# A's halves into the rows of G by transfers inside SBUF, and POOL's list in another order

## The chip, the cores and the metric

One core of a Trainium2 chip runs the kernel. The number compared is device time in microseconds of one execution on that core. The engines are PE (matrix products), DVE (vector), ACT (scalar), POOL (GpSimd) and SP, which here only issues DMA. Each has its own list of instructions in a fixed order, and they meet at semaphores.

## The reference

Two parts follow each other: a linear recurrence over 768 steps for 32 (batch, head) pairs with a 40 by 40 state, and a mixture of four causal attention experts on its output.

```python
for t in range(S):                       # S = 768, state is (B, H, 40, 40)
    y[:, :, t] = einsum('bhd,bhde->bhe', rt, state)
    Sa = einsum('bhde,bhe->bhd', state, at)
    state = state * wt[:, :, None, :] - einsum('bhd,bhe->bhde', Sa, bt)
    state = state + einsum('bhd,bhe->bhde', vt, kt)
...
logits = x @ w_gate                      # x is y, heads side by side; the two best of 4 experts per row
scores = (q @ k.T) / 8, causal           # per expert, then softmax, @ v, @ wo[e], weighted and summed
```

## The kernel before, in words

**The recurrence** takes 24 chunks of 32 steps. In a chunk the dependence between the steps is a triangular system per head: products of A (the input a times running decays) with KB (k and b over running decays) give a matrix G, and the part of G that couples the steps is inverted. Four chunks together are a wave, W = 0 to 5. A chunk's 32 heads are two units of sixteen heads, so a wave has 8 units and the recurrence 48. One turn n of the main loop (line 519) issues the stages g, k, f, p, u, y, v, t, d of units n, n-1 and n-2, in nine slots 0 to 8 (`MAIN`). After each slot come the extra jobs that the tables name for this turn and slot.

**Preparing a wave** (`prep`, table `SIDE`): a wave has 4 pieces, i = 4W + 0 to 3. In the table `2b` means step b of piece 2, a key is the turn relative to n0 = 8(W-1), and a slash goes to the next slot. The steps are a (scan of the decays into SUF, DVE), c and s (reciprocal and second scan into SC, DVE), x (A into AB, DVE), k or p (KB, on DVE or on POOL), m and n (G's products on PE and their masking by DVE into rows 0 to 63 of the tile GL), o (DMA of part of G to the scratch `Ld` in DRAM), d and q (the two halves of A into rows 64 to 103 of GL), and w, v, e (loads). Only piece 3 has its KB on POOL.

**Inverting a wave** (`invert`, table `INV`): L loads `Ld` back into MT in another layout, C writes a diagonal, T8 means eight operations of the elimination. Its 60 operations (30 products into TP, 30 sums into MT, L311) run on POOL alone for W = 1 to 5. A, D and E are DVE transposes of MT into TT (columns 0 to 15, 16 to 23 and 24 to 31). L stands in turn 8(W-1), E in turn 8W, and stage u of unit 8W is the first that reads wave W's TT.

**The order around the change.** L of wave W+1 stands on SP behind the o steps of turn 8W-1, two loads and four stores xT of the stage d of unit 8W-2. SP issues in order and keeps eight semaphores in turn for its transfers, so the ninth waits for the first to land. GL, MT and TT have two buffers each, AB four. The masking of step n, D, stage d and E stand on DVE in that order.

**After unit 47** the experts' part (`moe`, from about 375 us on) runs; the change touches nothing in it.

Of the kernel before, what the change touches and what calls it, by code (L numbers as in the profile page):

```python
# [8 lines left out]
AF = mybir.ActivationFunctionType  # L9
# [7 lines left out]
NW, NG, C = 6, 4, 32  # L17
# [16 lines left out]
    -6: "1b///0x//1k 0v 2ac//1we",  # L34
    -5: "///0m/1x 2s//1v",
    -4: "2b///1m/2k/2x/2we",
    -3: "///2m/3ac/3s 2v/3w",
    -2: "3b///0no 1no/3p/3x 3ve",
    -1: "///3m 2no 3no/0d///0q",
    0: "////1d////1q",  # L40
    2: "////2d",
    3: "////2q",
    4: "////3d",
    5: "////3q",
}

INV = {0: "L///////C", 1: "T8", 2: "T8", 3: "T8", 4: "T8", 5: "T8", 6: "T4/////A", 7: "T16/////D", 8: "E"}
INV1 = {0: "L C T10", 1: "T10", 2: "T10", 3: "T10", 4: "T10", 5: "T10", 6: "A", 7: "/////D", 8: "E"}


# [45 lines left out]
def recurrence(tc, ctx, I, xT, CM, early, tail=None):  # L96
    nc = tc.nc
# [4 lines left out]
    V, A, T, PL = nc.vector, nc.scalar, nc.tensor, nc.gpsimd  # L102
# [16 lines left out]
    def ring(name, shape, n):  # L119
        return [sp.tile(shape, F32, name=f"{name}{i}") for i in range(n)]  # L120

    A.dma_start(CM, I["CM"])
    def product():
        return ps([128, 4, 2, 32])
# [13 lines left out]
    GF = [ep.tile([128, 4098], F32, name="GLe")] + ring("GL", [128, 4098], 1)  # L138
    GL = [t[:, 0:4096].rearrange("p (g n s t) -> p g n s t", g=4, n=16, s=2) for t in GF]
# [29 lines left out]
    def load_e(i, k):  # L169
        if i < 24:  # L170
            t = (E8[i] if i < 8 else own[i % 2])[k]
            src, c0 = (("EA", 0), ("EA", 528), ("EK", 0))[k]
            nc.sync.dma_start(t[0:104], I[src][i, :, c0:c0 + t.shape[1]])

    def zero(t):
        p = t.start_partition()
        z = CM[p:p + t.shape[0], 194:195]
        for _ in t.shape[2:]:
            z = z.unsqueeze(1)
        A.activation(t, z.to_broadcast(t.shape), AF.Copy)  # L180
# [21 lines left out]
        PL.memset(t[:, 1024:1026], 0.0)  # L202

    def zgl(i):
        zero(GL[i][96:128].rearrange("p g n s t -> p (g n s t)"))

    def rest(x):
        if x < 2:
# [21 lines left out]
    def prep(i):  # L230

        w, g = divmod(i, NG)
        ab, sc, kb, pc = ABr[i % 4], SC[i % 12], KB[i % NKB], PC[i % 12]
        gl = GL[w % 2]
        SUF = SUFs[1 if i in (1, 3, 5, 7) else 0]
        sv = SUF[:, 1:529].rearrange("p (n c) -> p n c", c=33)
        EW, EA, EK = (x[0:104] for x in (E8[i] if i < 8 else own[i % 2]))
        ea = EA.rearrange("p (n c) -> p n c", c=32)
        def f0a():
            V.tensor_tensor_scan(SUF[:, 0:528][:, ::-1], EW[:, ::-1], d1[:, ::-1], 1.0, op0=OP.mult, op1=OP.add)  # L240
        def f0b():
            A.activation(pc, sv[:, ::4, 0], AF.Copy)
        def f0c():
            V.reciprocal(D1P[:, 0:528:132], sv[:, ::4, 0])
        def f1():
            V.tensor_tensor_scan(sc.rearrange("p n c -> p (n c)"), EW, D1P, 0.0, op0=OP.mult, op1=OP.add)  # L246
        aa = ab[0:104, 0:512].rearrange("p (n c) -> p n c", c=32)
        bd = ab[0:104].rearrange("p (s n c) -> p s n c", s=2, c=32)
        def f2():
            if i < 8:  # L250
                V.tensor_tensor(aa, ea, sc[:, :, 0:32], op=OP.mult)
                return
            for s in range(2):
                q = slice(64 * s, 64 * s + 40)
                V.tensor_tensor(bd[q, s], ea[q], sc[q, :, 0:32], op=OP.mult)
        def fk(e):
            e.tensor_tensor(kb[0:104].rearrange("p n (k c) -> p n k c", k=2), EK.rearrange("p (n k c) -> p n k c", n=16, k=2),  # L257
                             sv[:, :, None, 1:33].to_broadcast([104, 16, 2, 32]), op=OP.mult)
        def f5(s):
            o, q = gl[64:104, g, :, s, :], slice(64 * s, 64 * s + 40)  # L260
            a = aa[q] if i < 8 else bd[q, s]
            if True:
                A.activation(o, a, AF.Copy)
            else:
                PL.tensor_copy(o, a)
        def mm(c):
            p_a = product()
            o = gl[0:64, g].rearrange("q (p c) s t -> q p c s t", p=4)
            for p in range(4):
                for x in range(2):  # L270
                    n = p * 4 + c + x
                    if i < 8:
                        for s in range(2):
                            q = slice(64 * s, 64 * s + 40)
                            T.matmul(p_a[64 * s:64 * s + 64, p, x], kb[q, n, :], aa[q, n, :], start=True, stop=True, tile_position=(64 * s, 64 * s))  # L275
                    else:
                        T.matmul(p_a[64 * x:64 * x + 64, p], kb[0:104, n, :], bd[:, :, n], start=True, stop=True, tile_position=(0, 64 * x))  # L277
            for x in range(2):
                V.tensor_tensor(o[:, :, c:c + 2, x] if i < 8 else o[:, :, c + x], p_a[64 * x:64 * x + 64],
                                maskn[x][:, None, None, :].to_broadcast([64, 4, 2, 32]), op=OP.mult)  # L280
        def f6():
            for s in range(2):
                b = 64 * (g % 2) + 32 * s + 16 * (g // 2)
                nc.sync.dma_start(Ld[w % 2][b:b + 16].rearrange("n j t -> j n t"), gl[32:64, g, :, s])
        def load(k):
            load_e(i + (1 if k == 1 else 2), k)
        return dict(a=f0a, b=f0b, c=f0c, s=f1, x=f2, p=lambda: fk(PL), k=lambda: fk(V), d=lambda: f5(0), q=lambda: f5(1),
                    m=lambda: mm(0), n=lambda: mm(2), o=f6, w=lambda: load(0), v=lambda: load(1), e=lambda: load(2))

# [171 lines left out]
    for W in range(1, NW):  # L461
        n0 = 8 * (W - 1)
        inv = invert(W)
        for r, line in SIDE.items():
            if W == 1:
                break
            for k, part in enumerate(line.split("/")):
                for z in part.split():
                    at(n0 + r, 0 if n0 + r < 0 else k, *[P[4 * W + int(z[0])][x] for x in z[1:]])
                    if z[1] in "mn":  # L470
                        full.add(n0 + r)
        for r, line in (INV if W > 1 else INV1).items():
            for k, part in enumerate(line.split("/")):
# [5 lines left out]
    def seq(line):  # L479
        for z in line.split():  # L480
            if z[0] == "E":
                for k in (0, 2, 1)[:2 if z == "E9" else 3]:
                    load_e(int(z[1:]), k)
            elif z[0] == "Y":
                zero(ABr[int(z[1])][:, 0:512])
            elif z[0] == "W":
                rest(int(z[1]))
            elif z[0] == "Z":
                zgl(int(z[1]))
            elif z[0] == "V":  # L490
                for k in (0,) if z[2] == "0" else (2, 1):
                    load_c(int(z[1]), k)
            elif z[0] == "k":
                turned(0, int(z[1]))()
            elif z[0] == "g":
                units[int(z[1])]["g"]()
            elif z[0] in inv:
                inv[z[0]](*[int(x) for x in [z[1:]] if x])
            else:
                run(int(z[0]), z[1:])  # L500
# [18 lines left out]
    for n in range(NU + 2):  # L519
# [10 lines left out]
        for s, (x, d) in order:  # L530
            if x == "k":
                q, g = divmod(n + 2, 4)
# [466 lines left out]
```

## Time and profile before

| | |
|---|---|
| median of 3 runs | 611.88 us (607.84 to 613.04) |
| the profiled execution | 610.82 us, span 609.2 us |
| busy: PE / DVE / ACT / POOL | 515.2 / 430.9 / 426.9 / 370.5 us |
| main loop's turns 8 to 39 | about 129 to 335 us |
| DMA packets | 65230, of them 30440 under 512 B |

Times in a profile are microseconds from the start of the span. Below, list W is wave W's elimination on POOL, and E(W) the DVE transpose that closes it. In turn 8W-1 step m of piece 3 of wave W+1 is written 3m. The page's bytes per packet do not tell which transfers have short rows: here they are the o steps, whose rows are 128 bytes.

### The profile page before, as it was taken

The numbers are of one execution on the slowest core, as the hardware profiler recorded it, in microseconds if no ns is written. First come the engines' busy times: TensorE is split into PE (matmuls) and PEld (weight loads), VectorE is DVE, ScalarE is ACT, GpSimd is POOL, SyncE is SP. The second block draws the span as 40 slices with busy tenths as digits, with TensorE's granted clock in tenths as the row PEclk, the third lists the DMA queues.
The fourth block names the chain that finished last, engine by engine and source line by source line (L and its number), as shares of the span: only waits on it lengthen the run. The fifth ranks groups of instructions, "written<-read, shape, count | busy, mean of one in ns | idle before, by whom it ended". The sixth has DMA issues, their size and how long they took to land.

```text
span 609.2 us, 20123 instructions
## 1 busy us (share of the span) xinstructions
PE 515.2 (85%) x7985; PEld 441.8 (73%) x7985; DVE 430.9 (71%) x925; ACT 426.9 (70%) x1008; POOL 370.5 (61%) x597
## 2 busy tenths in 40 slices
PE   4656489988868868886998988799999999999996
PEld 4645377777757757675777777789887878897884
DVE  8666858889948966895665464787785677567752
ACT  6973167779839965893887774587776577677773
POOL 3412189818985994898488461486964566373841
PEclk9555578999969996997999999999999999999999
DMA  7864324577546646643632863442131132202101
GB/s 205 215 161 126 89 63 123 150 193 185 133 105 177 167 103 161 182 114 84 198 94 80 230 178 92 131 116 64 51 114 38 52 90 60 59 2 64 45 33 49
DMA packets 65230, 69.68 MB, mean 114 GB/s; under 512 B 30440, under 2 KB 51176, under 8 KB 65128
## 3 DMA queue, kind: packets, MB, share of 16 engines
q1 hardware_dynamic: 64984, 68.22, 41.9%
q8 instruction: 65, 1.06, 0.8%
q14 instruction: 37, 0.30, 0.2%
q10 hardware_dynamic: 144, 0.10, 0.1%
HBM read 50.99 MB, written 11.01 MB: 102 GB/s over the span
## 4 chain that ended last, share of the span: by engine, by line
PE 42%; POOL 26%; DVE 14%; issue 6%; ACT 5%; DMA 5%; SPq 1%; DVEq 0%; POOLq 0%; ACTq 0%
POOL MT L311 12%; POOL TP L311 11%; PE ot L875 6%; PE sc L829 5%; PE py L414 4%; PE pt L753 4%; PE pt L857 4%; DMA MT<-Ld 4%; PE pt L886 4%; PE pt L772 3%; PE pu L275 2%; PE pb L277 2%; PE pb L275 2%; PE pb L380 2%; DVE SC L246 1%
## 5 line engine op out<-in xcount | busy, mean ns | idle before, releaser
L311 POOL TENSOR_TENSOR MT<-MT,TP 128x30 f32<-128x30 f32 (+9 forms) x150 | 99.8, 665 | 11.8
L311 POOL TENSOR_TENSOR TP<-MT 128x30 f32<-128x30 f32 (+9 forms) x150 | 94.6, 631 | 11.1
L849 POOL TENSOR_TENSOR P<-P,m 128x128 f32<-128x128 f32 (+2 forms) x96 | 88.1, 939 | 3.4
L414 PE MATMUL py<-R,LS 128*40 128x80 f32 x1536 | 76.5, 242 | 4.6 <-DVE R L407 1.4
L838 ACT ACTIVATE P<-P,m 128x128 f32<-128x128 f32 (+2 forms) x96 | 63.8, 665 | 18.6 <-DVE m L836 14.0
L836 DVE CUSTOM_DVE_ANT_0 P<-sc,MK 128x128 f32<-128x128 f32 (+2 forms) x96 | 59.3, 623 | 23.1 <-PE sc L829 11.6
L414 PEld LDWEIGHTS py<-R,LS 128*40 128x40 f32 x1536 | 62.2, 121 | 16.5 <-ACT LS L443 9.2
L393 ACT ACTIVATE R<-pu 32x320 f32<-32x320 f32 x96 | 41.1, 428 | 42.7 <-PE pu L390 41.0
L829 PE MATMUL sc<-ks,qs 128*128 128x384 f32 (+4 forms) x256 | 61.0, 343 | 1.7 <-DVE m L836 1.6
L407 DVE TENSOR_TENSOR R<-pb,CM 64x256 f32<-64x256 f32 x96 | 40.3, 420 | 26.3 <-PE pb L404 20.4
L857 PE MATMUL pt<-CM,P 128*128 128x128 f32 x336 | 52.0, 275 | 0.9 <-ACT pt L863 0.4
L845 POOL TENSOR_TENSOR m<-m,gg 128x2 f32<-128x2 f32 x48 | 10.3, 215 | 69.5 <-DVE m L844 57.9
L363 ACT ACTIVATE LS<-pk 64x320 f32<-64x320 f32 x96 | 41.5, 432 | 8.9 <-PE pk L358 7.3
L857 PEld LDWEIGHTS pt<-CM,P 128*128 128x128 f32 x336 | 39.8, 140 | 6.0 <-ACT pt L863 1.5
L829 PEld LDWEIGHTS sc<-ks,qs 128*128 128x128 f32 x256 | 40.3, 189 | 4.4 <-DVE m L836 3.4
L753 PE MATMUL pt<-xh,wq 128*128 128x384 f32 x192 | 40.5, 344 | 2.6 <-DVE pt L861 1.2
L875 PE MATMUL ot<-pt,vv 128*64 128x256 f32 (+1 forms) x384 | 41.6, 359 | 0.1
L443 ACT ACTIVATE LS<-pt 40x320 f32<-40x320 f32 x92 | 39.6, 430 | 2.2
L863 ACT ACTIVATE pt<-pt 128x512 f32<-128x512 f32 (+1 forms) x64 | 34.3, 539 | 8.8 <-PE pt L857 7.8
L382 ACT ACTIVATE GT<-pb,OWN 128x160 f32<-128x160 f32 x96 | 32.4, 389 | 11.5 <-PE pb L380 10.9
L277 PE MATMUL pb<-AB,KB 104*64 104x64 f32 x512 | 25.4, 256 | 17.0 <-POOL KB L257 14.2
L404 PE MATMUL pb<-RB,VU 128*64 128x64 f32 x768 | 33.2, 230 | 4.2 <-ACT VU L399 3.2
(165 smaller groups left out, 1227.0 us busy)
## 6 DMA issues: line engine op xcount, KB each, us to landing
EK<-in_EK SPq DMA_DIRECT2D x20, 416.0 KB
ks<-ks SPq DMA_DIRECT2D x32, 192.0 KB
R<-in_VG SPq DMA_DIRECT2D x24, 208.0 KB
EW<-in_EA SPq DMA_DIRECT2D x20, 214.5 KB
R<-in_VT SPq DMA_DIRECT2D x48, 80.0 KB
R<-in_RT SPq DMA_DIRECT2D x24, 160.0 KB
RB<-in_RB SPq DMA_DIRECT2D x48, 80.0 KB
xT<-XT SPq DMA_DIRECT2D x48, 80.0 KB
```

The source lines that it names most:

```text
L311: return [lambda: e.tensor_tensor(tmp, row, col, op=OP.mult), lambda: e.tensor_tensor(o, o, tmp, op=OP.add)]
L363: A.activation(LS[(c + k) % 3][0:64, 8 * g:8 * g + 8], p_k[64 * k:64 * k + 64], AF.Copy)
L393: A.activation(r2[32:64, 40 * h0:40 * h0 + 640].rearrange("q (z p e) -> q z p e", z=2, p=2)[:, :, x], PU[64 * x:64 * x + 32, :, 0:160], AF ...
L407: V.tensor_tensor(o[:, :, x], p_f[64 * x:64 * x + 64], mask[x][:, None, None, :].to_broadcast([64, 4, 2, 32]), op=OP.mult)
L414: T.matmul(py[64 * s:64 * s + 40, p // 4, p % 4], ls[:, h, :], m, start=True, stop=True, tile_position=(0, 64 * s))
L753: T.matmul(p, w, x, start=(j == 0), stop=(j == len(prs) - 1))
L829: T.matmul(ps[:, c, 0:cw], QS[b][:, e, o], KS[b][:, e, z, k], start=(z == 0), stop=(z == 1))
L836: V.tensor_tensor_reduce(pv, ps[:, 0:ch, 0:cw], MK[:, 768 - n:768].rearrange("p (c k) -> p c k", c=ch), 1.0, 3e38, OP.add, OP.min, m[:, 0, ...
L838: later(DE, lambda: A.activation(P[:, 0:n], P[:, 0:n], AF.Exp, bias=m[:, 0, t:t + 1], scale=-1.0, accum_out=m[:, 1, t:t + 1]))
L849: PL.tensor_tensor(P[:, 0:n], P[:, 0:n], m[:, 3, t:t + 1].to_broadcast([128, n]), op=OP.mult)
L857: T.transpose(p[:, 128 * y:128 * y + 128], st["P"][t][:, 128 * c:128 * c + 128], ident)
L875: T.matmul(po[h, 128:256] if one else po[h], VV[b][:, k, 2 * ep + s], P[:, 256 * k:256 * k + (128 if one else 256)], start=(k == 0), stop= ...
```

## The change: what it does

Step d and step q of every piece from 8 on (two for each of 16 pieces, 32 in all) become one DMA each, from AB into rows 64 to 103 of GL, on SP, where ACT copied. Each moves 40 partitions of 16 rows of 32 floats, so 640 rows of 128 bytes. The two halves of a piece are issued together, in turns n0-1 to n0+2 instead of n0-1 to n0+5. KB of piece 3 moves from turn n0-2 to n0-3, and the elimination is dealt out in sevens and a nine. `zgl` writes the same region under another name for it.

```diff
@@ SIDE
-    -3: "///2m/3ac/3s 2v/3w",
-    -2: "3b///0no 1no/3p/3x 3ve",
-    -1: "///3m 2no 3no/0d///0q",
-    0: "////1d////1q",
-    2: "////2d",
-    3: "////2q",
-    4: "////3d",
-    5: "////3q",
+    -3: "///2m/3ac/3s 2v/3w/3p",
+    -2: "3b///0no 1no//3x 3ve",
+    -1: "///3m 2no 3no//0d 0q",
+    0: "/////1d 1q",
+    1: "/////2d 2q",
+    2: "/////3d 3q",
 }
-INV = {0: "L///////C", 1: "T8", 2: "T8", 3: "T8", 4: "T8", 5: "T8", 6: "T4/////A", 7: "T16/////D", 8: "E"}
+INV = {0: "L///////C", 1: "T7", 2: "T7", 3: "T7", 4: "T7", 5: "T7", 6: "T9/////A", 7: "T16/////D", 8: "E"}
@@ def zgl(i):
-        zero(GL[i][96:128].rearrange("p g n s t -> p (g n s t)"))
+        zero(GF[i][96:128, 0:4096])
@@ def f5(s):
             o, q = gl[64:104, g, :, s, :], slice(64 * s, 64 * s + 40)
-            a = aa[q] if i < 8 else bd[q, s]
-            if True:
-                A.activation(o, a, AF.Copy)
+            if i < 8:
+                A.activation(o, aa[q], AF.Copy)
             else:
-                PL.tensor_copy(o, a)
+                nc.sync.dma_start(o, bd[q, s])
```

On POOL, in the middle of list 2 (KB is the one product of EK and SUF; the last number of a row is its shape). Before:

```order
L311 TENSOR_TENSOR TP<-MT_121 128x234
L311 TENSOR_TENSOR MT_121<-MT_121,TP 128x18x13
...
L311 TENSOR_TENSOR MT_121<-MT_121,TP 128x22x9
L257 TENSOR_TENSOR KB_113<-EK_89,SUF_91 104x1024
L311 TENSOR_TENSOR TP<-MT_121 128x184
```

And now:

```order
L308 TENSOR_TENSOR TP<-MT_121 128x234
L255 TENSOR_TENSOR KB_113<-EK_89,SUF_91 104x1024
L308 TENSOR_TENSOR MT_121<-MT_121,TP 128x18x13
L308 TENSOR_TENSOR TP<-MT_121 128x228
...
L308 TENSOR_TENSOR MT_121<-MT_121,TP 128x22x9
L308 TENSOR_TENSOR TP<-MT_121 128x184
```

KB stood behind 44 of the 60 operations and stands behind 35. The same holds in lists 3 and 4. In list 1 all 60 stand ahead of KB in both kernels, and list 5 has no KB.

On SP, around the load of MT for wave 4 (Ld is step o, R and RB are inputs of the units, EW and EK of the next wave's pieces). Before:

```order
L284 DMA Ld_139<-GLe 32x16x32 x4
L345 DMA R_131<-in_VT 32x640
L343 DMA R_129<-in_VG 32x1664
L433 DMA xT<-XT_135 40x4x128 x4
L295 DMA MT_120<-Ld_139 128x1024
L347 DMA R_131<-in_VT 32x640
```

And now:

```order
L281 DMA Ld_139<-GLe 32x16x32 x4
L262 DMA GLe<-AB_114 40x16x32 x2
L342 DMA R_131<-in_VT 32x640
L340 DMA R_129<-in_VG 32x1664
L430 DMA xT<-XT_135 40x4x128 x4
L292 DMA MT_120<-Ld_139 128x1024
L262 DMA GLe<-AB_115 40x16x32 x2
L344 DMA R_131<-in_VT 32x640
```

The first pair of a wave stands between step o and the load of MT, the second right behind that load; the other two follow in the next two turns. PE's and DVE's orders stay as they were, and ACT's loses the 32 copies.

## Rows read from the trace of the kernel before

**Rows 1.** The page, section 4: the chain that ended last, by line.

```profile
POOL MT L311 12%; POOL TP L311 11%; PE ot L875 6%; PE sc L829 5%; PE py L414 4%; PE pt L753 4%; PE pt L857 4%; DMA MT<-Ld 4%; PE pt L886 4%; PE pt L772 3%; PE pu L275 2%; PE pb L277 2%; PE pb L275 2%; PE pb L380 2%; DVE SC L246 1%
```

**Rows 2.** Stretches: busy us of each engine, granted clock, DMA share, GB/s; units 16 to 23.

```profile
183.00:238.00 55.00, 45.52 (x942) 38.01 (x939) 43.09 (x72) 41.08 (x97) 43.11 (x62) 0.91 0.58 146
```

**Rows 3.** Waits: engine, line waited for, us in total, times, longest.

```profile
PE pb L277 <- POOL KB L257: 14.2, 3, 5.0
```

**Rows 4.** The chain of waits, 218 to 246 us: start, us, what.

```profile
227.30 2.13 POOL KB L257
...
233.46 2.31 PE py L414 x32
...
239.61 4.63 DMA MT<-Ld
...
244.28 0.16 POOL MT L297
```

**Rows 5.** The chain of waits, 121 to 136 us, one wave earlier.

```profile
121.60 0.69 PE pb L277 x16
...
124.63 1.26 PE py L414 x32
...
130.71 4.59 DMA MT<-Ld
```

**Rows 6.** Timeline of PE: start, us, instruction, [idle before <-releaser]; two starts of 3m.

```profile
174.64 1.98 PE L277 MATMUL pb<-AB,KB 104*64 104x64 f32 x32 [4.96 <-POOL KB L257]
...
229.48 1.98 PE L277 MATMUL pb<-AB,KB 104*64 104x64 f32 x32 [4.95 <-POOL KB L257]
```

**Rows 7.** Timeline of POOL: ends of lists and starts of lists.

```profile
135.34 0.15 POOL L297 MEMSET MT<- 128x32 f32 x1 [13.81 <-DMA MT<-Ld]
...
164.86 0.61 POOL L311 TENSOR_TENSOR TP<-MT 128x234 f32<-128x234 f32 x1
...
181.99 0.26 POOL L311 TENSOR_TENSOR MT<-MT,TP 128x30 f32<-128x30 f32 x1
...
189.82 1.32 POOL L311 TENSOR_TENSOR MT<-MT,TP 128x30 f32<-128x30 f32 x1
...
291.28 0.26 POOL L311 TENSOR_TENSOR MT<-MT,TP 128x30 f32<-128x30 f32 x1
299.03 0.16 POOL L297 MEMSET MT<- 128x32 f32 x1 [7.49 <-DMA MT<-Ld]
...
334.22 0.27 POOL L311 TENSOR_TENSOR MT<-MT,TP 128x30 f32<-128x30 f32 x1
```

**Rows 8.** Timeline of DVE: E(2), SUF of piece 3, two maskings, E(4), E(5).

```profile
182.99 0.65 DVE L313 STREAM_TRANSPOSE TT<-MT 128x256 f32<-128x256 f32 x1
...
214.22 1.26 DVE L240 TENSOR_TENSOR_SCAN SUF<-EW,D 104x528 f32<-104x528 f32 x1
...
218.11 0.86 DVE L407 TENSOR_TENSOR R<-pb,CM 64x256 f32<-64x256 f32 x2 [0.58 <-PE pb L404]
...
224.65 0.42 DVE L407 TENSOR_TENSOR R<-pb,CM 64x256 f32<-64x256 f32 x1 [0.64 <-PE pb L404]
...
292.28 0.65 DVE L313 STREAM_TRANSPOSE TT<-MT 128x256 f32<-128x256 f32 x1
...
334.52 0.63 DVE L313 STREAM_TRANSPOSE TT<-MT 128x256 f32<-128x256 f32 x1 [1.29 <-POOL MT L311]
```

**Rows 9.** Timeline of SP: the step o ahead of the load of MT for wave 2.

```profile
124.42 2.04 SPq L284 DMA_DIRECT2D Ld<-GLe  x4
```

**Rows 10.** L263, the copies: engine, count, ns min/median/max, first and last start.

```profile
L263 ACT ACTIVATE GLe<-AB x24: 626/627/631, 10.1 to 269.3; 40x512 f32<-40x512 f32 x24
```

**Rows 11.** Stretches: with four transfers of step o alone, and after a stall of PE.

```profile
165.00:169.00 4.00, 3.66 (x85) 2.96 (x75) 3.86 (x7) 3.23 (x8) 3.69 (x5) 1.00 0.44 77
229.00:236.00 7.00, 6.33 (x99) 5.59 (x100) 2.73 (x7) 2.35 (x5) 6.06 (x14) 0.50 0.65 147
```

**Rows 12.** The chain of waits, 60 to 75 us: landing of step o.

```profile
65.87 1.87 DMA Ld<-GL
```

## The prediction

> **What bounds the kernel now.** I read the chain of waits first. Its two longest lines are the elimination on POOL [rows 1], so in the recurrence it is the lists that must be followed, not the busiest engine: in units 16 to 23 no engine is busy for more than 46 of 55 us [rows 2]. The chain between 218 and 246 us shows why a wave takes about 55 us. POOL reaches KB at 227.30, behind 44 operations; PE's 3m starts when KB is done; the load of MT is issued at 239.61, and the next list starts at 244.28 [rows 4]. The table of waits says what the units lose there: PE waits for this KB three times, 14.2 us in all [rows 3], in lists 2, 3 and 4. PE's timeline dates it: 3m was ready at 174.64 - 4.96 = 169.68 and at 229.48 - 4.95 = 224.53 [rows 6]. The last views are POOL's and DVE's timelines, for a second bound behind the first. List 2 runs from 135.34 to 182.25, and E(2) starts at 182.99, only 0.74 us later; list 4 ends at 291.54 and E(4) starts at 292.28 [rows 7, 8]. E needs the last operation of its list, and unit 8W's stage u needs E. So the units arrive when POOL has just finished. Once E did wait: E(5), 1.29 us for POOL [rows 8].
>
> **The change, part by part.**
>
> *KB earlier.* Nothing is saved on POOL; KB and its 60 operations remain, in another order. After the memset of list 2 the 35th operation ended at 165.47, that is 30.1 us later [rows 7]; KB takes 2.13 [rows 4], so it would be done 32.3 us after a list starts, in list 2 at about 167.6, ahead of the 169.68 at which 3m wants it. PE's wait goes, in all three lists. What is late next is E: units that come 5 us earlier meet a list that ends no earlier.
>
> *The path after it.* It goes through every second wave: list 2, E(2), units 16 to 23, load, list 4, E(4), units 32 to 39, E(5). Its terms, all from rows:
> - List 2 starts at 135.34 and lasts 46.91, KB included, wherever in it KB stands [rows 7].
> - The wait for its semaphore and E itself, 0.05 + 0.65 = 0.70 [rows 8].
> - From the end of E(2), 183.64, to 3m ready, 224.53: 40.9 [rows 6, 8].
> - From 3m to the load of MT: 9.11, from 121.60 to 130.71, where PE had not been stalled [rows 5]. Behind the stall it is 10.13 today [rows 4, 6].
> - From the load's issue to the memset of list 4: 4.65 [rows 4, 5].
> - List 4 lasts 291.54 - 244.28 = 47.26 [rows 4, 7]; then 0.70 again.
> - From the end of E(4), 292.93, to where E(5) wants to run, 334.52 - 1.29 = 333.23: 40.3 [rows 8].
>
> These add up to 325.87 for the start of E(5), against 334.52: **8.65 us earlier, before costs**. Lists 3 and 5 are beside this path: list 5 starts at least when list 4 ends, where today POOL idles 7.49 us for the load [rows 7], so its end moves further forward than the units do and E(5) no longer waits.
>
> *PE's clock.* With E late, PE idles before stage u of units 16 and 32 instead of before 3m. After today's stall of 4.95 us the granted clock is 0.50 from 229 to 236 us [rows 11], its lower level, 1.2 GHz, and stage y takes 2.31 us there against 1.26 at full clock [rows 4, 5]. It could cost nothing if the waits come out shorter, or about 2 us if a second stage y falls into it. I take 1.05 for each of the two waits: **2.1**.
>
> *The 32 transfers.* A piece's pair has 2 x 640 = 1280 rows of 128 bytes. Step o moves such rows: four transfers, 2048 rows, filled 0.44 of 4 us of the 16 DMA engines, 1.76 us [rows 11]. The pair at that rate is 1.1 us of all engines. On SP it adds two issues of 2.04 / 4 = 0.51 us [rows 9]. The first pair of a wave stands between step o and the load of MT. It could delay that load by nothing, where SP waits for the XT of stage d anyway, or by two issues and two whole landings of 1.87 us [rows 12], 4.8 us. I take 1.1, since the nearest row is that of step o. The path holds two such loads, of waves 2 and 4: **2.2**. The second pair is issued behind the load and should not slow it; the other pairs have two turns or more before AB is written again.
>
> By the Trainium skill's "DMA: Bandwidth & Descriptors", section "Specifications", rows under 512 bytes fall to read-modify-write and lose the line rate. The 128-byte rows of step o agree in so far as they go at 256 KB in 1.76 us, 149 GB/s. If a write into SBUF paid twice what step o pays, the pair would be 2.2 us and the sum 2.2 us worse; no row here shows such a write.
>
> *KB beside DVE's scans.* In list 3 KB would be reached at about 184.5 + 30.1 = 214.6 (3m at 169.68, then 9.11, 1.1 and 4.65), but SUF of piece 3 ends 31.84 us after E(2) [rows 8], at 184.05 + 31.84 + 1.05 = 216.9. So POOL waits some 2 us, harmless beside 7 us of slack, and KB then starts just ahead of DVE's second scan of that piece. A POOL operation that takes 0.27 us alone took 1.32 beside a two-input operation of DVE [rows 7]: the two engines hold each other up. The scan may lose nothing, or nearly all of KB's 2.13. DVE waits 0.58 and 0.64 for PE later in the same stretch [rows 8] and wins these back, so I take 2.13 - 0.2 (its head start) - 1.2: **0.7**.
>
> The Trainium skill's "SBUF — State Buffer", section "Who interferes with whom", has it harder: VectorE with two SBUF inputs and GpSimd take a shared port in turn, and whoever starts first keeps it for its whole instruction. The 1.32 agrees. By that alone, with nothing won back, the sum would be 1.2 us worse.
>
> *ScalarE's copies.* 32 copies of 627 ns [rows 10] go, 20.1 us of ACT. ACT is busy 41 of 55 us [rows 2] and the path above runs through POOL, DVE and PE; I count **nothing**. The units' dependence hides it; if ACT alone were the path, it would be worth up to 20 us.
>
> **Sum:** 8.65 - 2.1 - 2.2 - 0.7 = 3.65 us. The profiled execution took 610.82 (span 609.2, 1.6 around it) and would take 607.2; it lies 1.06 under the median of the runs, 611.88, so I forecast **608.2**.
>
> **Rivals.**
> - *The costs don't arise.* The pairs drain while SP waits for XT, PE's clock holds, DVE loses nothing: 611.88 - 8.65 = 603.2, with a little left 604. For it: each of the three bounds above reaches down to nothing. Against it: PE idled about as long today and its clock did fall. 22%.
> - *The list is no bound, and all three waits are won:* 611.88 - 14.2 = 597.7; also if ACT's 20 us lie on the path. Against it: E(5) waited for POOL, and E(2) and E(4) start 0.74 us after their lists. 5%.
> - *The wait only changes its name.* E takes the whole of it and the clock the rest: 611.9. 10%.
> - *Slower: the first pair in front of the load of MT.* The place is SP between step o and that load, the price 4.8 us or more instead of 1.1, paid in waves 2 and 4. 8.65 - 2.1 - 0.7 - 9.5 = -3.7: 615.5. It decides from 2.9 us per load; over 1% needs 6. For it: DMA is busy for 0.65 of the stretch in which the load is issued [rows 11], and the pair's rows are short. Against it: step o's own rows. 13%.
>
> By the Trainium skill's rule on short rows alone ("DMA: Bandwidth & Descriptors", section "Specifications") this last case is half way reached, 2.2 of 4.8 us; the rows of step o, which are as short, keep it at 13%.
>
> The forecast itself, 606 to 611, has 50%.
>
> **The numbers.** About 1%, 6.1 us, is what a measurement of this kernel can tell from no change. Faster by more: the first two rivals and the forecast's edge, 0.30. Slower by more: the worse part of the last, 0.08. The rest, 0.62. The range, 602 to 613.5, takes in the whole gain at its low end and a delay of 3.5 us per load at its high end.
>
> **What would show it.** In the profile after: PE's wait for KB gone; instead DVE's L313 waits for POOL 4 to 7 us ahead of E(2) and E(4) and 1 to 3 ahead of E(3); list 4 starting 2 to 4 us earlier than 244.28; ACT down by 20 us; a slow-clock stretch of PE behind E(2). I am wrong if E never waits, if the load of MT is issued later than 9 to 11 us after 3m, or if a load's landing grows well beyond 4.6 us.

## The result: no gain, half a per cent slower

The changed kernel takes 614.73 us (median of 14 runs, 611.41 to 619.81), the kernel before 611.89 in the same comparison: ratio 1.0052, interval 1.0026 to 1.0077. The forecast was 608.2, with a range up to 613.5. Medians are of all runs, ratios and intervals of the fast runs alone, so a ratio need not be the quotient of two medians. The profiled execution after took 612.1 us, its span 610.3; it lies 2.6 under the median. Lines of the changed kernel are numbered two or three lower: L308 is the elimination on POOL, L310 the transposes D and E, L255 KB, L238 SUF, L253 AB, L262 the transfers, L292 the load of MT.

The page after, its busy times (share of the span, instructions), and the first entries of the chain that ended last by line:

```profile
PE 514.9 (84%) x7985; PEld 442.9 (73%) x7985; DVE 432.3 (71%) x925; ACT 406.6 (67%) x976; POOL 365.1 (60%) x597
...
PE ot L872 6%; PE sc L826 5%; PE pt L750 4%; PE pt L854 4%; PE py L411 4%; PE pt L883 4%; POOL MT L308 4%; POOL TP L308 3%; PE pt L769 3%; PE pb L377 2%; DVE R L423 2%; ACT LS L440 1%; DVE P L833 1%; ACT GT L379 1%; DMA MT<-Ld 1%
```

ACT fell by 20.3 us, the 32 copies. The two elimination lines held 23% of the chain before [rows 1] and hold 7% now: for most of the recurrence the list has stopped being what is waited for. The table of waits after (engine, line waited for, us, times, longest) says what took its place. PE's wait for KB [rows 3] is not in it. E's wait for its list has grown from 1.3 us, and the waits for two loads are new (before, 0.4 and 0.8 us):

```profile
DVE TT L310 <- POOL MT L308: 7.9, 2, 5.1
DVE AB L253 <- DMA EA<-in_EA: 7.7, 6, 3.1
DVE SUF L238 <- DMA EW<-in_EA: 4.5, 3, 2.3
```

DVE now waits for the loads of the pieces' inputs, EW and EA. Its timeline shows the two largest of list 3:

```profile
200.45 1.29 DVE L238 TENSOR_TENSOR_SCAN SUF<-EW,D 104x528 f32<-104x528 f32 x1 [2.25 <-DMA EW<-in_EA]
...
206.84 1.90 DVE L253 TENSOR_TENSOR AB<-EA,SC 40x512 f32<-40x512 f32 x2 [2.69 <-DMA EA<-in_EA]
```

Why the loads are late stands in SP's timeline (start, us, line, transfer). First the kernel before, in the turn behind E(2), then the changed kernel in the same turn:

```profile
187.97 1.72 SPq L433 DMA_DIRECT2D xT<-XT  x4
190.33 0.33 SPq L173 DMA_DIRECT2D EW<-in_EA  x1
...
197.53 0.31 SPq L173 DMA_DIRECT2D EA<-in_EA  x1
```

```profile
187.54 0.35 SPq L292 DMA_DIRECT2D MT<-Ld  x1
187.94 1.66 SPq L262 DMA_DIRECT2D GL<-AB  x2
189.70 2.63 SPq L344 DMA_DIRECT2D R<-in_VT  x1
192.38 0.34 SPq L345 DMA_DIRECT2D R<-in_RT  x1
192.77 0.70 SPq L349 DMA_DIRECT2D RB<-in_RB  x2
193.57 1.70 SPq L430 DMA_DIRECT2D xT<-XT  x4
195.32 1.63 SPq L262 DMA_DIRECT2D GL<-AB  x2
197.05 0.64 SPq L171 DMA_DIRECT2D EW<-in_EA  x1
...
199.08 1.63 SPq L262 DMA_DIRECT2D GL<-AB  x2
200.81 3.19 SPq L171 DMA_DIRECT2D EA<-in_EA  x1
```

From 187.54 to 197.05 SP does nothing but issue, without a gap longer than 0.1 us. A transfer takes 0.8 us of SP, a pair 1.63 to 1.66 here. The issue behind two of the pairs then does not return: the load of VT takes 2.63 us and that of EA 3.19, where such issues mostly take 0.31 to 0.34. These are the second pair, right behind the load of MT, and the fourth, behind EW and EK. In waves 2 to 4 the issues behind these two took 2.0 to 3.2 us, those behind the first and third pair 0.50 to 0.72. SP did not wait for one of its eight semaphores: from 120 to 340 us, landings held it for 0.5 us in all. EW is issued 6.7 us later than before and EA 3.3 us; 2.8 us of the 6.7 are there already at the load of MT (184.78 before). In the chain of waits after (start, us, what), EW's landing is a link. So are, further on, the issues of the first pair of wave 4 and the load of MT for list 4, which lands later than the 4.63 of [rows 4]:

```profile
197.05 3.27 DMA EW<-in_EA
...
235.06 1.12 SPq L262
236.23 0.78 SPq L262
...
239.96 6.07 DMA MT<-Ld
```

### The profile page after: what moved, and what is told of

Same layout as the page of the kernel before. It is cut to its first block, busy times and chain, and to the rows that moved or that the text cites. A ratio compares the mean times of both kernels' runs of the same rounds, so it can differ in the third digit from the quotient of the medians.

```text
span 610.3 us, 20129 instructions
## 1 busy us (share of the span) xinstructions
PE 514.9 (84%) x7985; PEld 442.9 (73%) x7985; DVE 432.3 (71%) x925; ACT 406.6 (67%) x976; POOL 365.1 (60%) x597
## 4 chain that ended last, share of the span: by engine, by line
PE 36%; DVE 9%; POOL 8%; ACT 5%; issue 4%; DMA 3%; SPq 3%; DVEq 0%; ACTq 0%; POOLq 0%
PE ot L872 6%; PE sc L826 5%; PE pt L750 4%; PE pt L854 4%; PE py L411 4%; PE pt L883 4%; POOL MT L308 4%; POOL TP L308 3%; PE pt L769 3%; PE pb L377 2%; DVE R L423 2%; ACT LS L440 1%; DVE P L833 1%; ACT GT L379 1%; DMA MT<-Ld 1%
## 5 line engine op out<-in xcount | busy, mean ns | idle before, releaser
L308 POOL TENSOR_TENSOR MT<-MT,TP 128x30 f32<-128x30 f32 (+9 forms) x150 | 93.6, 624 | 11.5
L308 POOL TENSOR_TENSOR TP<-MT 128x30 f32<-128x30 f32 (+9 forms) x150 | 93.5, 623 | 11.4
L411 PE MATMUL py<-R,LS 128*40 128x80 f32 x1536 | 78.9, 246 | 11.3 <-ACT R L390 3.7
L411 PEld LDWEIGHTS py<-R,LS 128*40 128x40 f32 x1536 | 64.5, 124 | 23.5 <-ACT LS L440 7.5
L421 ACT ACTIVATE R<-py 40x320 f32<-40x320 f32 x48 | 20.7, 431 | 24.4 <-PE py L411 24.2
```

The source lines that it names most:

```text
L308: return [lambda: e.tensor_tensor(tmp, row, col, op=OP.mult), lambda: e.tensor_tensor(o, o, tmp, op=OP.add)]
L411: T.matmul(py[64 * s:64 * s + 40, p // 4, p % 4], ls[:, h, :], m, start=True, stop=True, tile_position=(0, 64 * s))
```

## The experiments

Each ratio is against the kernel before, run beside it; times from different comparisons are set against each other by ratio, where 0.001 is 0.61 us.

**The list's order alone.** The new places of KB and of the elimination's operations, with the copies on ACT in their old turns.

```diff
-    -3: "...3w",        -2: "3b///0no 1no/3p/3x 3ve",    T8 ... T4
+    -3: "...3w/3p",     -2: "3b///0no 1no//3x 3ve",      T7 ... T9
```

> Before, with KB of piece 3 one turn earlier and the elimination dealt in sevens and a nine; the 32 copies stay on ScalarE in their old turns. Theory T (the transfers hold SP: each pair's issue takes 1.6 us and the next issue up to 3.2 us, so the loads EW and EA of the next pieces land late and DVE waits 11.4 us for them in lists 2 to 4): without transfers the list's earlier KB is worth what the prediction's sum gives without its transfer term, 8.65 - 2.1 - 0.7 = 5.9 us, so about 606 us, ratio 0.990; no wait of DVE for EW or EA beyond before's. Rival L (POOL's list takes the whole gain, the transfers cost nothing): within 1 us of before, ratio 1.000, with DVE waiting at E for all that was won.

606.6 us, 0.9911 (0.9875 to 0.9946): 5.4 us faster, as expected. Its timeline of DVE, E(2), E(4) and E(5), answering to [rows 8]:

```profile
182.80 0.63 DVE L313 STREAM_TRANSPOSE TT<-MT 128x256 f32<-128x256 f32 x1 [6.31 <-POOL MT L311]
...
287.48 0.63 DVE L313 STREAM_TRANSPOSE TT<-MT 128x256 f32<-128x256 f32 x1 [5.23 <-POOL MT L311]
...
328.86 0.65 DVE L313 STREAM_TRANSPOSE TT<-MT 128x256 f32<-128x256 f32 x1
```

E waits for POOL as the forecast had it (4 to 7 us; E(3) 2.50), and E(5) starts 5.7 us earlier than before.

**The transfers alone**, in the copies' old turns, with the list as before.

```diff
-    A.activation(o, a, AF.Copy)
+    nc.sync.dma_start(o, bd[q, s])        # pieces from 8 on
```

> Before, with the 32 transfers in place of the copies in the copies' old turns, one or two a turn over seven turns; KB and the elimination as before. Theory T: single transfers hold SP half as long at a time, but the load waits appear and the wait for KB stays, part of them in parallel with it: 2 to 6 us slower, ratio 1.003 to 1.010. Rival L: as before or up to 1 us faster, ratio 0.998 to 1.000.

614.55 us, 1.0032 (1.0008 to 1.0056): slower, as expected. So the two halves of the change have opposite signs.

**The transfers on ACT's queue**, all else as changed (`A.dma_start` for `nc.sync.dma_start`).

> The changed kernel, with the 32 transfers issued by ScalarE's queue instead of SP. Theory T, if it is SP's issue time that delays the loads: SP is as free as before, so DVE's waits for EW and EA go (under 3 us of the 11.4 are left) and the time is near e_list, about 607 us, ratio 0.992; ScalarE is held 0.8 us per transfer, about what the copy took. Rival Q (it is the traffic of 20480 short rows on the DMA engines, whoever issues it): the waits stay within 2 us of the 11.4 and the time is near the changed kernel, ratio 1.003 to 1.006.

634.1 us, 1.0371 (1.0329 to 1.0412): missed. SP's issue of VT behind the load of MT was back at 0.34 to 0.46, but POOL waited 82.7 us for the loads of MT (55.5 in the changed kernel) and DVE 19.7 us for EW. The transfers of both queues take the same eight semaphores in turn, so SP now waits for what ACT issues late (it waited 10.7 us for one such transfer ahead of a load of MT). That run says nothing on the price of the transfers.

**The third and fourth pair later** in their turns, behind the issues of EW and EK (slot 8 for slot 5).

> The changed kernel, with the third and fourth pair of a wave moved to the end of their turn, so that on SP they stand behind EW and EK of that turn instead of ahead of them. Theory T: EW lands about 2 us earlier (its wait, 1.4 and 2.3 us in lists 2 and 3, goes); EA of piece 1 is still behind a pair, so 2 to 4 us better than the changed kernel, ratio to before 0.999 to 1.003. Rival Q: no change from the changed kernel, ratio 1.005.

612.85 us, 1.0000 (0.9968 to 1.0033), as expected: 3.2 us of the loss come back from the place in SP's order alone, though the interval just touches the changed kernel's.

**Copies in the transfers' turns.** The changed kernel with ACT's copies for the transfers; and two halves of it: only the first pair of a wave as transfers, only the other three.

```diff
-    nc.sync.dma_start(o, bd[q, s])
+    A.activation(o, bd[q, s], AF.Copy)    # all / g > 0 / g == 0
```

> The changed kernel with ScalarE's copies in place of the 32 transfers, in the changed kernel's turns: the two differ in the transfers alone. Theory (the transfers cost the 8 us, the new order of the list gains 5): 606 to 608, ratio 0.990 to 0.994, no wait of DVE for EW and less than 2 us of waits for EA, E waits some 14 us. Rival (the copies' new turns beside the new list cost it, not the transfers): 612 to 615, ratio above 1.000.

> Only the first pair of each wave is a transfer, the other three are copies by ScalarE. This is the pair that the prediction charged with 1.1 us per load of MT. Theory: SP's issue behind a pair blocks wherever the pair stands, so the first pair delays only the load of MT, by some 1 to 2 us in waves 2 and 4: 608 to 610, ratio 0.994 to 0.998, no wait of DVE for EW. Rival (the first pair is the one that costs, as the slower rival of the prediction had it): 613 to 615, ratio above 1.002.

> The first pair of each wave is copied by ScalarE, the other three are transfers: the pairs that the prediction priced at nothing. Theory: they keep SP, and the rings, in front of the loads of EW and EA, so DVE's waits for EW and EA (11 us in lists 2 to 4) stay: 611 to 613.5, ratio 0.999 to 1.003. Rival (the first pair is the one that costs): 606 to 609, ratio 0.990 to 0.995.

612.7 us, 1.0020 (0.9993 to 1.0046); 616.17, 1.0060 (1.0027 to 1.0093); 610.01, 0.9962 (0.9939 to 0.9985). The first two came out as their rivals had it, and the third between both. All-copies was meant as the ground to measure transfers from, and it is none: two copies in a row cost too. ACT's timeline, PE's, and a stretch of PE (busy us of each engine, granted clock, DMA share, GB/s) in the kernel with copies:

```profile
194.75 1.26 ACT L262 ACTIVATE GL<-AB 40x512 f32<-40x512 f32 x2
196.04 0.59 ACT L396 ACTIVATE VU<-pb 80x512 f32<-80x512 f32 x1
```

```profile
196.68 1.12 PE L401 MATMUL pb<-RB,VU 128*64 128x64 f32 x16 [2.02 <-ACT VU L396]
```

```profile
196.00:202.00 6.00, 5.32 (x72) 4.52 (x73) 3.97 (x5) 3.38 (x10) 5.45 (x8) 0.50 0.29 57
```

VU stands behind the two copies, PE waits 2.02 us for it, and its granted clock is then 0.50 for six microseconds. With the copies spread out this stretch ran at 1.00 (the kernel with the list alone). The profiled execution with copies took 617.02 us, 4.3 above its median. So these three were no clean test, and the next ones leave the work out. Set against them, three pairs of copies cost 9.1 us in these turns (1.0060 to 0.9911): the second kernel is slow by its copies, not by its first pair.

**Neither copies nor transfers**, then the first pair alone, then the other three alone. They leave out A's halves in G for the pieces concerned.

```diff
-            else:
+            elif False / g == 0 / g > 0:
                 nc.sync.dma_start(o, bd[q, s])
```

> The changed kernel with neither the 32 transfers nor copies in their place; what is left out is A's halves in G for the sixteen-head units. It gives the new list's order with ScalarE freed and nothing on SP. Theory (ScalarE's copies, spread as they were before the change, hide; the transfers alone cost the 8 us): 605 to 608, as the list's order gave by itself (606.6), ratio 0.988 to 0.993. Rival (each copy stands ahead of VU on ScalarE, so freeing ScalarE is worth something, and the transfers cost more than 8 us): 600 to 604, ratio 0.980 to 0.987.

> As the kernel without any of them, but with the first pair of each wave as transfers; the other pairs are left out. Theory (the pairs behind the load of MT carry the cost, through EW and EA): 1 to 3 us above the kernel without any. Rival (the first pair, ahead of the load of MT, carries it): 4 us or more above it.

> As the kernel without any of them, but with the second to fourth pair of each wave as transfers; the first pair is left out. Theory (these pairs carry the cost, through EW and EA): 4 to 7 us above the kernel without any, DVE's waits for EA some 5 us or more. Rival (the first pair carries it): 0 to 2 us above it.

| kernel | median | ratio | interval |
|---|---|---|---|
| neither | 604.63 | 0.9868 | 0.9829 to 0.9907 |
| first pair only | 607.11 | 0.9911 | 0.9882 to 0.9941 |
| the other three only | 611.32 | 0.9976 | 0.9947 to 1.0005 |
| all four: the changed kernel | 614.73 | 1.0052 | 1.0026 to 1.0077 |

The first pair costs 0.0043, 2.6 us, a difference within both intervals. The other three cost 0.0108, 6.6 us, which is clear. Together they cost 11.3 us, 2.1 more than the two parts. In the trace of the other three DVE waits 4.3 us for EA, a little under what was expected; that execution took 606.43 us, 4.9 under its median. It also shows that a pair holds the next issue without another pair ahead of it (wave 2, the pair right behind the load of MT, and VT):

```profile
131.03 1.80 SPq L262 DMA_DIRECT2D GLe<-AB  x2
132.94 2.43 SPq L344 DMA_DIRECT2D R<-in_VT  x1
```

The timelines of DVE show where. D and E of waves 2 to 5, the changed kernel:

```profile
182.15 0.67 DVE L310 STREAM_TRANSPOSE TT<-MT 128x256 f32<-128x256 f32 x1
...
183.18 0.65 DVE L310 STREAM_TRANSPOSE TT<-MT 128x256 f32<-128x256 f32 x1
...
234.69 0.66 DVE L310 STREAM_TRANSPOSE TT<-MT 128x256 f32<-128x256 f32 x1
...
238.59 0.63 DVE L310 STREAM_TRANSPOSE TT<-MT 128x256 f32<-128x256 f32 x1 [2.81 <-POOL MT L308]
...
287.13 0.66 DVE L310 STREAM_TRANSPOSE TT<-MT 128x256 f32<-128x256 f32 x1
293.30 0.63 DVE L310 STREAM_TRANSPOSE TT<-MT 128x256 f32<-128x256 f32 x1 [5.08 <-POOL MT L308]
...
335.36 0.65 DVE L310 STREAM_TRANSPOSE TT<-MT 128x256 f32<-128x256 f32 x1
```

The kernel with neither (there L308 is the transposes, L306 the elimination):

```profile
175.51 0.66 DVE L308 STREAM_TRANSPOSE TT<-MT 128x256 f32<-128x256 f32 x1
...
182.93 0.63 DVE L308 STREAM_TRANSPOSE TT<-MT 128x256 f32<-128x256 f32 x1 [6.32 <-POOL MT L306]
...
230.20 0.67 DVE L308 STREAM_TRANSPOSE TT<-MT 128x256 f32<-128x256 f32 x1
...
234.26 0.62 DVE L308 STREAM_TRANSPOSE TT<-MT 128x256 f32<-128x256 f32 x1 [2.96 <-POOL MT L306]
...
281.32 0.67 DVE L308 STREAM_TRANSPOSE TT<-MT 128x256 f32<-128x256 f32 x1
...
286.70 0.63 DVE L308 STREAM_TRANSPOSE TT<-MT 128x256 f32<-128x256 f32 x1 [4.28 <-POOL MT L306]
...
328.03 0.64 DVE L308 STREAM_TRANSPOSE TT<-MT 128x256 f32<-128x256 f32 x1
```

D waits for nothing in these rows, so its start says when the units arrive. In wave 2 they arrive 6.6 us later with the transfers (DVE's waits for loads there sum to 4.8 us); E(2) hides that from the units behind it, since the list ends no earlier. It is not hidden from the load of MT for list 3, which does not wait for E(2): that list starts 9.2 us later and ends 4.3 later, and E(3), which waits for it in both kernels, is 4.3 later too. The list's first row on POOL, the changed kernel and the one with neither:

```profile
193.17 0.15 POOL L294 MEMSET MT<- 128x32 f32 x1 [10.21 <-DMA MT<-Ld]
```

```profile
183.98 0.15 POOL L292 MEMSET MT<- 128x32 f32 x1 [1.08 <-DMA MT<-Ld]
```

From E(2) to the next D it is 51.5 us against 47.3, beside 5.1 us of waits for loads; from E(3) on 48.5 against 47.1, beside 1.4. E(5) starts 7.3 us later, and the two profiled spans differ by 6.8. The other 4.5 of the 11.3 us lie between these two executions and the medians, and stand in no trace.

**One transfer at a time.** The new list with the transfers in the copies' old turns; and the changed kernel with the two halves of a pair three slots apart.

```diff
     # the first: f5 of the changed kernel, SIDE's d and q as before
     # the second:
-    -1: "...//0d 0q",    0: "/////1d 1q",     and so for 2, 3
+    -1: "...//0d///0q",  0: "/////1d///1q",   and so for 2, 3
```

> The new order of the list, and the transfers, issued one at a time in the turns in which the copies stood before the change, in place of two in one turn. Theory (1280 rows block the next issue, and single transfers with a turn between them leave the rings time to drain): issues behind them near 1 us or less, DVE's waits for EW and EA under 5 us in lists 2 to 4, 607 to 610.5, ratio 0.992 to 0.998. Rival (each transfer costs the same wherever it stands): 612 to 616, ratio above 1.000.

> The changed kernel with the two transfers of a pair three places apart in the same turn, so that other issues of SP stand between them; all else as changed. Theory (two transfers in a row fill what SP can hand over, and the issue behind them blocks): 608 to 611.5, ratio 0.993 to 0.999, the issue behind a transfer under 1.5 us. Rival (the turns themselves are the cause, since the loads of EW and EA stand behind them in any case): 613 to 616, ratio above 1.001.

608.58 us, 0.9925 (0.9898 to 0.9953), and 608.15, 0.9947 (0.9922 to 0.9973): the transfers are the same 32, and 7.8 and 6.4 us of the 11.3 are gone. The rivals fall. In the second, one number was missed: where a q of one pair still meets the d of the next, EA's issue blocks as long as before. DVE waits 8.0 us for EA there, no less than in the changed kernel (7.7), and 1.6 for EW in place of 4.5; so the waits for EA are not simply time of the kernel. Its SP:

```profile
197.12 1.63 SPq L262 DMA_DIRECT2D GL<-AB  x2
198.86 3.00 SPq L171 DMA_DIRECT2D EA<-in_EA  x1
```

**Rows or bytes.** The changed kernel with the same bytes in 40 rows of 2 KB; and with 640 rows of 4 bytes.

```diff
-    nc.sync.dma_start(o, bd[q, s])
+    nc.sync.dma_start(GF[w % 2][64:104, 1024 * g + 512 * s:1024 * g + 512 * s + 512], ab[q, 512 * s:512 * s + 512])
+    # or
+    nc.sync.dma_start(o[:, :, 0:1], bd[q, s][:, :, 0:1])
```

> The changed kernel with each transfer's 80 KB as 40 rows of 2 KB in place of 640 rows of 128 bytes; what is left out is the order of A's halves within their rows of G. Theory (the number of rows counts: they fill the rings, and the next issue on SP blocks): issue behind a pair back to about 0.35 us, no wait for EW, under 2 us for EA, 606 to 609, ratio 0.990 to 0.996. Rival (the bytes, or a write into SBUF, or just two more issues count): 611 to 615, ratio above 0.999.

> The changed kernel with one number (4 bytes) of each of the 640 rows of a transfer in place of 128 bytes; what is left out is 31 of 32 of A's numbers. As many rows as the changed kernel, a 32nd of the bytes; the kernel with 40 rows of 2 KB has the same bytes and a 16th of the rows (608.9 us). Theory (what counts is rows): it stays where the changed kernel is, 612 to 616, ratio 1.000 to 1.007, issues on SP still 0.75 us or more and the issue behind a pair over 1.5 us. Rival (a short row is dear by its bytes or what is read and written back with them): 606 to 610, ratio 0.990 to 0.997.

608.9 us, 0.9948 (0.9922 to 0.9974), and 610.54, 1.0010 (0.9980 to 1.0040). Fewer rows at the same bytes give back 6.4 us, a 32nd of the bytes at the same rows 2.6, which is within both intervals: mostly rows. No run has as many rows of 512 bytes or more, so their number and their shortness are not told apart. The median of the second is 1.5 us below what was expected, its ratio inside. SP with long rows, and with 4-byte rows, at the fourth pair of wave 2, where EA follows the pair at once:

```profile
144.28 1.51 SPq L262 DMA_DIRECT2D GLe<-AB  x2
145.89 0.47 SPq L171 DMA_DIRECT2D EA<-in_EA  x1
```

```profile
145.70 1.64 SPq L262 DMA_DIRECT2D GLe<-AB  x2
147.44 3.20 SPq L171 DMA_DIRECT2D EA<-in_EA  x1
```

The issue of a transfer costs about as much with 40 rows (0.74 us) as with 640 (0.80); the block behind the second and the fourth pair goes with the rows (0.41 to 0.47 with 40, where it follows at once).

**A better version: KB on DVE.** The kernel before with piece 3's KB on DVE, in its old turn; copies and list as before.

```diff
-    -2: "3b///0no 1no/3p/3x 3ve",
+    -2: "3b///0no 1no/3k/3x 3ve",
```

> A candidate: the kernel before with piece 3's KB on DVE in place of POOL, in its old turn, POOL's list as before the change, ScalarE's copies as before. The list is 2.13 us shorter and KB no longer stands behind it. If the list still bounds a wave (E waited for POOL 14 us in the kernel with the new list alone, 606.6): two lists on the path, 4 us less than that kernel, 602 to 605, ratio 0.984 to 0.990. If DVE, busy 43 of 53 us there, pays for it with 1.3 us a wave: 605 to 608, ratio 0.989 to 0.994. If KB held POOL and DVE up already as it was: no gain over the kernel before.

601.49 us, 0.9859 (0.9831 to 0.9887), the lowest median of all and a little under the expected time, its ratio inside. E(2) and E(5) there:

```profile
180.34 0.63 DVE L313 STREAM_TRANSPOSE TT<-MT 128x256 f32<-128x256 f32 x1 [3.04 <-POOL MT L311]
...
325.25 0.64 DVE L313 STREAM_TRANSPOSE TT<-MT 128x256 f32<-128x256 f32 x1
```

E(2) comes 2.46 us earlier than with the new list alone, about the 2.13 that KB took on POOL. E(5) is 3.6 earlier, and the 1.2 to 1.3 us that KB takes on DVE are not seen.

## Why the prediction was wrong

**The step that failed** is "The second pair is issued behind the load and should not slow it; the other pairs have two turns or more before AB is written again." The later three pairs were priced at nothing and cost 6.6 us. The sentence asks only who waits for the transfer itself: the load of MT, and the next writer of AB. It does not ask what is queued behind it on SP. There stand VT, xT, EW and EA, and EW and EA have little slack: in the kernel before, EW was issued 7.3 us behind E(2) and DVE had no wait for it, while 6.7 us later DVE waits 2.25. That the loss lies in the pairs and in their place on SP is shown by leaving them out and by moving them; that all 6.6 us go through EW and EA is not shown.

**A price was also too low.** The pair's issue was taken from step o's four, 0.51 us each [rows 9]. It is 0.8. That the issue behind a pair blocks, for 2.0 to 3.2 us behind the second and fourth, has no row in the trace of before. Step o was no guide to it, though its rows are as short: the VT behind it took 1.13 us at most.

**What held.** Without the transfers the sum was 8.65 - 2.1 - 0.7 = 5.85 us of gain; the list alone gave 5.4 (3.3 to 7.6), an interval too wide to test the single terms. PE's wait for KB went, and E waited in its place. In the changed kernel E(3) waits 2.81 and E(4) 5.08, as forecast, and E(2) not at all, since the units come late. The clock fell in the place foreseen: stage y behind E(2) takes 2.37 us in the kernel with the list alone (granted clock 0.53 from 184 to 190 us),

```profile
184.26 2.37 PE L414 MATMUL py<-R,LS 128*40 128x80 f32 x32
```

against 1.26 at full clock [rows 5]; behind E(4) it takes 2.37 again. That is 2.2 us for the two, where 2.1 were taken.

**The first pair** was charged 2.2 us for two loads, and the runs give 2.6 (by the two intervals anything from nothing to some 6). So the slower rival, the same pair at 4.8 us per load, is not what happened, though the time came out near its 615.5: most of what cost was SP's work behind the load of MT, not ahead of it. That 2.6 lies near 2.2 is partly luck. With the first pair alone it is 16.8 us from 3m to the start of list 4, against 13.8 with neither: a load is held up 3.0 us, not 1.1, and the lists take part of it back (list 2 lasts 44.5 us in place of 47.0). In the changed kernel the load of MT for list 4 was issued 0.35 us later than before [rows 4] and took 1.44 longer to land; list 4 started at 246.07, not 2 to 4 us earlier than 244.28. A landing well beyond 4.6 was one of the signs named for being wrong.

**KB beside DVE's scans** was charged 0.7 us in list 3. There POOL waited 1.56 us, until SUF was done (the profile names a product of PE as releaser), as foreseen (some 2). But the scan started first, by 0.19 us, and no scan was held: KB took 3.05 us in place of 2.18. So this term fell on nothing in list 3. A scan was held in list 2, where DVE came late after its waits for EW and EA. DVE's scan, then POOL:

```profile
165.42 3.18 DVE L244 TENSOR_TENSOR_SCAN SC<-EW,D1P 104x528 f32<-104x528 f32 x1
```

```profile
165.30 2.18 POOL L255 TENSOR_TENSOR KB<-EK,SUF 104x1024 f32<-104x1024 f32 x1 [1.25 <-PE pb L395]
```

Such a scan takes 1.26 us [rows 8] and here, started 0.12 us behind KB, loses 1.9, KB's time less a little. The rule of the Trainium skill's "SBUF — State Buffer", section "Who interferes with whom", that the first to start keeps the shared port, agrees with both.

**ScalarE's copies at nothing.** Taking them away from the new list gives 0.9911 to 0.9868, 2.6 us, within both intervals. If they cost, it is little as long as they stand apart; two in a row, in the transfers' turns, cost 6.7 us (0.9911 to 1.0020).

**Rows.** In this kernel 640 short rows inside SBUF are dear, by the 6.4 us that 40 long ones give back. The Trainium skill's "DMA: Bandwidth & Descriptors", section "Why small descriptors are slow (HBM only)", says that transfers from SBUF to SBUF don't suffer from small descriptors. The measurement differs for what stands behind them on the issuing queue; the rate of such a transfer itself, of which the page speaks, no row here gives. The Trainium skill's section "Specifications" of the same page, on rows under 512 bytes, was weighed in the prediction by the bytes' rate. With a 32nd of the bytes most of the loss stays, so the rate is not it; a price per short row would fit both runs.

**What stays open**: what exactly holds the issue behind a pair. It goes with the rows, with two transfers in a row, and with a load of MT, or of EW and EK, just ahead of them; a queue of rows that is full would fit, but no run here reads such a queue. Nor is it settled why all four pairs cost 2.1 us more than their parts.

## What to carry to other kernels

When a copy moves from an engine to a DMA, list what stands behind that DMA on its queue until the next load somebody waits for, and charge it the issue and the block behind it, not only the transfer. Spread such transfers: the same 32 cost 3.5 us instead of 11.3 one at a time in the copies' old turns, which is still no better than ACT's copies there (0.9925 against 0.9911). When a list bounds a stage, try taking work out of it (KB on DVE, 1.4%) before reordering it (0.9%; the two intervals overlap a little).

## What the runs showed of the hardware

- One DMA of 640 rows of 128 bytes takes 0.8 us of SP; of 640 rows of 4 bytes 0.8, and of 40 rows of 2 KB 0.74. A load of 32 or 104 rows mostly takes 0.31 to 0.34.
- Behind two DMAs of 640 rows that followed the load of MT, or of EW and EK, the next issue took 2.0 to 3.2 us in the changed kernel (4.5 once, with the first pair copied); behind two that followed stores, 0.50 to 0.72; behind two of 40 rows, 0.41 to 0.47.
- Of a scan on DVE with two inputs and KB on POOL, the one that started second lost: the scan took 3.18 us in place of 1.26 (0.12 us behind KB), KB 3.05 in place of 2.18 (0.19 us behind the scan).
- A wait of PE of 2.02 us, ahead of one stage, was followed by a stretch at the lower clock, granted 0.50, in the changed kernel's list with copies. What this stretch alone cost no run shows.
